# Layer 1's seven-product blocks: readers of another engine's sums issued later, weight sums and splits issued earlier

## The chip, the cores and the metric

One core of a Trainium2 chip. The metric is the device time of one execution in microseconds; the time before is the median of three runs. The profile is of one execution, taken by the hardware profiler.

## The reference

Attention with a hash mask over q, k, v (2 x 8 heads, 768 tokens, 64 wide), then two feed-forward layers in float32. What the change touches is the first of them:

```python
gate = 1.0 / (1.0 + np.exp(-(x @ w_gate)))   # x: 1536 x 512, w_gate: 512 x 1536
val = x @ w_val                               # w_val: 512 x 1536
return (gate * val @ w_out)                   # w_out: 1536 x 512
```

The second layer computes h = x @ w_in, g = h * cos(h), and g @ w_out. All weights arrive as float64.

## The kernel before

**Numbers.** A float32 product is made of three matmuls on rounded parts (high x high, high x low, low x high). So each operand is split: ScalarE casts the high part (L120), and VectorE or GpSimd subtracts it from the operand (L121, the tiles that end in `l`). `convert_parts` turns a weight's float64 words into float32: a ScalarE multiplication (L148, `wp`) and three VectorE instructions (L150, L154, L164).

**Layer 1.** The 1536 hidden columns are 12 blocks f of 128, the tokens three chunks c of 512 (tiles `xy`). g and v are the gate's and the value's weights, o and z the output weights of the two layers. Blocks 0 and 1 are computed plainly (items `in`). The other ten are taken in pairs p = 1 to 5 (f = 2p and 2p+1): for g and then for v, chunks 0 and 1 of both blocks come from seven products M1 to M7 instead of eight, and chunk 2 from two plain ones, P0 and P1. The nine steps follow in the order M1 M5 M2 M6 M3 P0 M7 P1 M4. M1 to M4 read tokens (M4 reads chunk 1's first half, which has been overwritten by a sum), M5, M6, M7 read sums of tokens (tiles T1, T2, T3) and sums of weights (`s12`, `s34`; split tiles `s0..`, `s1..`). Each product is six matmuls of 512 columns, P0 and P1 are twelve. Steps P0 and P1 of g are followed by an `out` item each (twelve matmuls, `a<-gh/gl,o_..`), which multiplies the finished chunk 0 of the pair before with its output weights.

**After a product.** `step` adds a product to running sums: M1 and M5 are copied out of PSUM by ScalarE; c11 = M2 + M1; u = M6 + M1; q = u + M5, then q + M3; u + M7, then M5's tile + u (GpSimd); u + M4. Each finished sum goes to `gate` (ScalarE's sigmoid) for g, or to `value` for v (L836: VectorE multiplies it with the gate). Names in the profile: `M1tg`, `M5tv`, `qg` are these sums; `g<-P1v,g` is `value` reading a product in PSUM.

**Buffers.** The products go round four PSUM banks (`bank`): a step needs the bank of the step four before it, that is its reader. Split weights have four buffers for each role.

**Order.** The program is recorded item by item and keeps that order on every engine; each engine runs its queue in order. `due[n]` lists what is issued ahead of item n: conversions, splits (`wsplit`, `ssplit`), weight sums (`wsum`, GpSimd), loads, spills, and the splits of finished chunks for the output items (`gsplit`, tiles `gh`, `gl`). `before(n, mm)` gives the item that lies mm matmuls ahead of n, `lead` these distances for a weight: first that of its conversion, then that of its split.

**Layer 2** is computed plainly (`PLAIN[2] = 8`). After the items with c = 0 each layer has passes over its output items for c = 1 and 2, with chunks that were spilled to DRAM and are fetched again.

Of the kernel before, what the change touches and what calls it, by code (L numbers as in the profile page):

```python
# [39 lines left out]
def lsh_attention_glu_moe_cos_moe(  # L40
# [663 lines left out]
    def moe():  # L704
        with ExitStack() as st:
# [32 lines left out]
            def wsum(nm, p):  # L738
                w0, w1 = wt.pop((nm, 2 * p, 0)), wt.pop((nm, 2 * p + 1, 0))
# [19 lines left out]
            t4 = {}  # L759
# [7 lines left out]
            def tsplit(h, lw, src, sub):  # L767
                split(h, lw, src, sub)

            def tsum3(l, k, eng, sub):  # L770
                a, b = temp(f"ta{l}{k}"), temp(f"tb{l}{k}")
                eng.tensor_tensor(out=a, in0=x32(1, 0, 2 + k), in1=x32(1, 0, k), op=ALU.subtract)
                eng.tensor_tensor(out=b, in0=x32(1, 1, 2 + k), in1=x32(1, 1, k), op=ALU.subtract)
                eng.tensor_tensor(out=a, in0=a, in1=b, op=ALU.add)
                split(tt[l, 3][:, 0, k, :], tt[l, 3][:, 1, k, :], a, sub)

            def tsum1(l, k, eng, sub):
                a, b = temp(f"tc{l}{k}"), temp(f"td{l}{k}")
                eng.tensor_tensor(out=a, in0=x32(1, 0, k), in1=x32(0, 0, k), op=ALU.subtract)
                eng.tensor_tensor(out=b, in0=x32(1, 1, k), in1=x32(0, 1, k), op=ALU.subtract)  # L780
                eng.tensor_tensor(out=a, in0=a, in1=b, op=ALU.add)
                split(tt[l, 1][:, 0, k, :], tt[l, 1][:, 1, k, :], a, sub)
                eng.tensor_tensor(out=b, in0=x32(1, 0, 2 + k), in1=a, op=ALU.subtract)
                eng.tensor_tensor(out=b, in0=b, in1=x32(1, 1, 2 + k), op=ALU.add)
                split(tt[l, 2][:, 0, k, :], tt[l, 2][:, 1, k, :], b, sub)
                eng.tensor_tensor(out=a, in0=x32(0, 0, 2 + k), in1=b, op=ALU.subtract)
                eng.tensor_tensor(out=a, in0=a, in1=x32(0, 1, 2 + k), op=ALU.add)
                t4[l, k] = a

            def tsum4(l, k, sub):  # L790
                split(xy[1][:, 0, k, :], xy[1][:, 1, k, :], t4.pop((l, k)), sub)
# [76 lines left out]
            st_t = {}  # L868

            def step(n, name, l, nm, p, fill):  # L870
# [37 lines left out]

                if name in ("M1", "M5"):
                    st_t[name] = temp(f"{name}t{nm}{p}")  # L910
                    nc.scalar.copy(st_t[name], ps)
                elif name == "M2":
                    t = temp(f"c11{nm}{p}")
                    plus(nc.vector, t, ps, st_t["M1"])
                    after(t, f0, 0)
                elif name == "M6":
# [3 lines left out]
                    plus(nc.gpsimd, t, u, st_t["M5"])  # L920
                elif name == "M3":
                    t = st_t["q"]
                    plus(nc.vector, t, ps, t)
                    after(t, f0, 1)
                elif name == "M7":
# [3 lines left out]
                    after(t, f1, 1)  # L929
                elif name == "M4":  # L930
                    u = st_t["M1"]
                    plus(nc.vector, u, ps, u)
                    after(u, f1, 0)
# [78 lines left out]
            release = dict(split_at)  # L1012
            for n, (kind, l, f, c) in enumerate(items):
# [10 lines left out]
                elif kind == "M1":  # L1024
                    m = before(n, 36)
                    for f_ in (2 * c, 2 * c + 1):
                        release[f, f_, 0] = m
                    assert all(split_at[f, x, 0] <= m for x in (2 * c, 2 * c + 1))
            for kk in sorted(order, key=lambda kk: begin[use[kk]] - lead(kk)[1]):
                due[split_at[kk]].append(lambda kk=kk: wsplit(kk))  # L1030
            for n, (kind, l, f, c) in enumerate(items):
# [97 lines left out]
```

## Time and profile before

| | |
|---|---|
| median of 3 runs | 889.86 us (885.63 to 890.15) |
| the profiled execution | 892.29 us, its span 890.5 us |
| TensorE busy, in the span | 811.0 us (91%) |
| VectorE | 671.6 us (75%) |
| ScalarE | 489.0 us (55%) |
| GpSimd | 442.5 us (50%) |
| mean granted TensorE clock | 0.966 of full |

The first 270 us are attention; the c = 0 items of the first layer follow to about 538 us, its output passes to about 613, and the second layer to the end. Matmuls are pipelined and their ends are modelled, so a busy TensorE is not one at its peak. An engine's share is a mean over stages that have different limits.

### The profile page before, as it was taken

What the parts mean: (1) busy time and instruction counts of PE and PEld (TensorE: products, weight loads), DVE (VectorE), ACT (ScalarE), POOL (GpSimd) and SP (SyncE); (2) the same over time, 40 slices, a digit from 0 to 9 for tenths busy, and PEclk for the clock granted to TensorE, in tenths of its full rate; (3) what the DMA queues carried; (4) which work ended last, traced back from release to release, by engine and by line L of the source; (5) the groups of instructions that cost most, each with busy time, mean ns of one, the idle gap of its engine ahead of it and who ended that gap; (6) DMA issues with size and microseconds to landing.
All of it is one profiled execution on the core that took longest, in us unless ns stands there. A gap on an engine that the chain in (4) does not pass through costs nothing.

```text
span 890.5 us, 12055 instructions
## 1 busy us (share of the span) xinstructions
PE 811.0 (91%) x3924; PEld 675.5 (76%) x3924; DVE 671.6 (75%) x1060; ACT 489.0 (55%) x944; POOL 442.5 (50%) x409
## 2 busy tenths in 40 slices
PE   6999999999998597787979799999899999989997
PEld 4998889888986485575757577887788888867885
DVE  6999999999965656666666648778777777777774
ACT  5888878888963243242332243445566666654443
POOL 5778877978657576474747452222222222212221
PEclk8999999999998899899989799999999999999999
DMA  6887666676211132313232324553444444447552
GB/s 150 193 222 154 161 163 166 164 168 157 64 27 36 48 107 64 102 48 121 68 119 71 119 71 166 194 177 104 142 145 148 150 147 143 153 168 250 199 177 95
DMA packets 85199, 118.44 MB, mean 133 GB/s; under 512 B 31312, under 2 KB 53840, under 8 KB 85136
## 3 DMA queue, kind: packets, MB, share of 16 engines
q1 hardware_dynamic: 80352, 112.75, 43.5%
q10 hardware_dynamic: 4784, 4.92, 1.8%
q8 instruction: 31, 0.51, 0.2%
q14 instruction: 32, 0.26, 0.1%
HBM read 74.45 MB, written 17.83 MB: 104 GB/s over the span
## 4 chain that ended last, share of the span: by engine, by line
PE 55%; DVE 26%; POOL 7%; issue 5%; ACT 5%; DMA 1%; SPq 0%; DVEq 0%; POOLq 0%; ACTq 0%
PE ph L810 13%; PE a L991 13%; PE a L964 7%; DVE mn L447 4%; PE t L505 4%; DVE pl L515 3%; PE s L436 2%; PE s L439 2%; PE o L526 2%; PE o L525 2%; DVE gl L121 2%; DVE g L836 2%; DVE wl_o L154 1%; DVE w_o L164 1%; DVE w_v L164 1%
## 5 line engine op out<-in xcount | busy, mean ns | idle before, releaser
L489 POOL TENSOR_SCALAR p<-p,r,d 128x768 f32<-128x768 f32 x96 | 97.0, 1015 | 45.8 <-DVE r L480 35.5
L510 ACT CAST ph<-t 128x384 fp32r<-128x384 f32 x192 | 92.4, 485 | 26.2 <-PE t L505 18.0
L515 DVE TENSOR_TENSOR pl<-t,ph 128x384 fp32r<-128x384 f32 x192 | 99.5, 545 | 5.0 <-ACT ph L510 3.4
L447 DVE TENSOR_REDUCE mn<-s 128x1 f32<-128x768 f32 x96 | 90.8, 946 | 10.8 <-PE s L439 10.7
L505 PE MATMUL t<-ident,p 128*128 128x128 f32 x576 | 95.4, 274 | 1.3 <-POOL p L489 1.0
L454 ACT ACTIVATE p<-s,mn 128x768 f32<-128x768 f32 x96 | 87.8, 914 | 6.4 <-DVE mn L447 6.0
L505 PEld LDWEIGHTS t<-ident,p 128*128 128x128 f32 x576 | 74.9, 141 | 10.1 <-DVE bf L400 2.0
L525 PE MATMUL o<-ph,vs 128*128 128x384 f32 x192 | 78.9, 411 | 0.3 <-ACT e L534 0.3
L120 ACT CAST gh<-r 128x512 fp32r<-128x512 f32 x56 | 34.8, 622 | 79.8 <-PE a L991 45.0
L436 PE MATMUL s<-k,q 96*128 96x384 f32 x192 | 71.9, 374 | 2.2 <-ACT p L454 1.6
L526 PE MATMUL o<-pl,vs 128*128 128x384 f32 x192 | 66.3, 345 | 2.5 <-DVE pl L515 2.0
L439 PE MATMUL s<-k,q 128*128 128x384 f32 x192 | 66.6, 347 | 0.0
L843 ACT ACTIVATE n<-ph,quarter 128x512 int32<-128x512 f32 x48 | 33.0, 687 | 59.9 <-PE ph L810 59.7
L121 DVE TENSOR_TENSOR gl<-r,gh 128x512 fp32r<-128x512 f32 x56 | 41.8, 747 | 29.6 <-ACT gh L120 29.5
L845 DVE SCALAR_TENSOR_TENSOR g<-ph,n 128x512 f32<-128x512 f32 x48 | 33.1, 690 | 21.7 <-ACT n L843 21.6
L851 DVE TENSOR_TENSOR g<-ph,g 128x512 f32<-128x512 f32 x48 | 33.0, 688 | 16.9 <-ACT g L850 16.9
L526 PEld LDWEIGHTS o<-pl,vs 128*128 128x128 f32 x192 | 36.8, 191 | 5.9 <-DVE pl L515 5.8
L436 PEld LDWEIGHTS s<-k,q 96*128 96x128 f32 x192 | 37.6, 196 | 3.5 <-ACT p L454 2.7
L850 ACT ACTIVATE g<-g,halfpi 128x512 f32<-128x512 f32 x48 | 34.6, 720 | 7.8 <-DVE g L845 7.8
L525 PEld LDWEIGHTS o<-ph,vs 128*128 128x128 f32 x192 | 36.8, 192 | 1.7 <-ACT e L534 1.7
L439 PEld LDWEIGHTS s<-k,q 128*128 128x128 f32 x192 | 37.7, 196 | 0.0
L154 DVE SCALAR_TENSOR_TENSOR wl_o<-wp_o,wl_o 128x512 int32<-128x512 int32 x24 | 19.6, 819 | 17.8 <-ACT wp_o L148 16.1
(927 smaller groups left out, 2419.2 us busy)
## 6 DMA issues: line engine op xcount, KB each, us to landing
raw_z<-in_moe_w_out SPq DMA_DIRECT2D x32, 512.0 KB, 3.8
d<-g SPq DMA_DIRECT2D x56, 256.0 KB, 3.3
r<-d SPq DMA_DIRECT2D x56, 256.0 KB, 4.0
raw_o<-in_moe_w_out SPq DMA_DIRECT2D x22, 512.0 KB, 3.4
q<-x SPq DMA_DIRECT2D x45, 192.0 KB, 3.1
k<-x SPq DMA_DIRECT2D x45, 192.0 KB, 3.4
raw_i<-in_moe_w_in SPq DMA_DIRECT2D x16, 512.0 KB, 4.3
raw_v<-in_moe_w_val SPq DMA_DIRECT2D x9, 512.0 KB, 3.5
```

Source lines behind the costliest of these rows:

```text
L436: nc.tensor.matmul(o, hh["q2"][0:96, t, :], hh["k2"][0:96, sl, :], start=True, stop=False)
L439: nc.tensor.matmul(o, hh["q1"][:, t, :], hh["k1"][:, sl, :], start=False, stop=True)
L447: nc.vector.tensor_reduce(mn_t[u][:, i : i + 1], s_t[g], axis=AX.XY, op=ALU.min)
L454: nc.scalar.activation(pt, s_t.pop(g), AF.Exp, bias=mn_t[u][:, i : i + 1], scale=-1.0, accum_out=sm_t[u][:, i : i + 1],)
L489: nc.gpsimd.tensor_scalar(out=pt, in0=pt, scalar1=r[:, i : i + 1], scalar2=d[:, i : i + 1], op0=ALU.mult, op1=ALU.add,)
L505: nc.tensor.transpose(pt[:, i, :], pv_[:, j * P : (j + 1) * P], ident)
L510: nc.scalar.copy(ph, pt_t[w])
L515: nc.vector.tensor_tensor(out=pl, in0=pt_t.pop(w), in1=ph_t[w].bitcast(F32), op=ALU.subtract)
L525: nc.tensor.matmul(o_t[u], vs[:, j, :], ph_t.pop(w), start=(j == 0), stop=False)
L526: nc.tensor.matmul(o_t[u], vs[:, j, :], pl_t.pop(w), start=False, stop=(j == T - 1))
L810: nc.tensor.matmul(ps, w[:, kt, :], xy[c][:, hl, kt, :], start=(n == 0), stop=(n == 11))
L991: nc.tensor.matmul(acc[c, t], m[:, ts], w, start=(f == 0 and n == 0), stop=(f == F2 - 1 and n == 2),)
```

## The change

1. **Readers later** (`after` with `wait`, `far`, `post`): the gate of M2, M3, M4 is issued one item later; the gate or value of M7's second sum, which GpSimd adds, three items later.
2. q = u + M5 is added by VectorE instead of GpSimd.
3. **Weights earlier**: conversions of paired weights lead by 150 or 138 matmuls (before 120, 108, 90, 78), splits by 84 or 60 (before 52, 44), weight sums by 100 (36), their splits by 72 and 48 (30, 22). The split of a weight releases its tile now, the sum only reads it.
4. Conversions are put first in each item's list (`early`), in both layers.
5. The sums of tokens (`tsums`) are issued in four stages at items of their own, the splits of a stage after the sums of it, for the two halves k = 0 (GpSimd) and k = 1 (VectorE).

```diff
         if paired(key):
             odd = f % 2
-            return (120 - 12 * odd if nm in "gv" else 90 - 12 * odd), 52 - 8 * odd
+            return 150 - 12 * odd, (60 if odd else 84)
...
-                w0, w1 = wt.pop((nm, 2 * p, 0)), wt.pop((nm, 2 * p + 1, 0))
+                w0, w1 = wt[nm, 2 * p, 0], wt[nm, 2 * p + 1, 0]
...
+                return (
+                    (sum3, sum1),
+                    (lambda: parts(3), sum2),
+                    (lambda: parts(1), lambda: parts(2), sum4),
+                    (lambda: parts(4),),
+                )
...
-                def after(src, f, c):
+                def after(src, f, c, wait=0):
                     if nm == "i":
                         cosine(n, src, f, c, fill)
+                    elif wait:
+                        post.setdefault(n + wait, []).append(lambda: use_it(n + wait, src, f, c))
                     else:
                         use_it(n, src, f, c)
...
+                far = int(nm == "g")
...
-                    after(t, f0, 0)
+                    after(t, f0, 0, far)
...
-                    plus(nc.gpsimd, t, u, st_t["M5"])
+                    plus(nc.vector, t, u, st_t["M5"])
...
                     plus(nc.gpsimd, t, u, t)
-                    after(t, f1, 1)
+                    after(t, f1, 1, 3)
...
+            for n, (kind, l, f, c) in enumerate(items):
+                if kind == "M1":
+                    due[before(n, 100)].append(lambda f=f, c=c: wsum(f, c))
+                    due[before(n, 72)].append(lambda f=f, c=c: ssplit(f, c, 0))
+                    due[before(n, 48)].append(lambda f=f, c=c: ssplit(f, c, 1))
...
-                due[n].append(lambda k=k: convert_to(k + 1))
+                m = before(use[kk], 100) if paired(kk) else split_at[kk]
+                assert n <= m, (kk, n, m, order[k - NEARLY])
+                early[n].append(lambda k=k: convert_to(k + 1))
+            due = [a + b for a, b in zip(early, due)]
...
+                    if l == 1:
+                        slots = (6, 7, 8, 9) if k else (3, 5, 7, 9)
...
+                    for fn in post.pop(n, ()):
+                        fn()
```

**First place: VectorE at the end of the second pair and in g of the third.** Rows are in the order of issue; names as above, the last numbers being the program's. Before, from the sum of M7v to the split of an output item's chunk:

```order
L907 TENSOR_TENSOR M1tv_5003<-M7v_5109,M1tv_5003 128x512
L836 TENSOR_TENSOR g_1_5_4949<-M5tv_5012,g_1_5_4949 128x512
L150 TENSOR_SCALAR wl_v_5124<-raw_v_5071 128x512
L154 SCALAR_TENSOR_TENSOR wl_v_5124<-wp_v_5122,wl_v_5124 128x512
L164 SCALAR_TENSOR_TENSOR w_v_5127<-raw_v_5071,wl_v_5124 128x512
L836 TENSOR_TENSOR g_2_5_4972<-P1v_5130,g_2_5_4972 128x512
L907 TENSOR_TENSOR M1tv_5003<-M4v_5146,M1tv_5003 128x512
L836 TENSOR_TENSOR g_0_5_4994<-M1tv_5003,g_0_5_4994 128x512
L907 TENSOR_TENSOR c11g_5185<-M2g_5178,M1tg_5167 128x512
L907 TENSOR_TENSOR M1tg_5167<-M6g_5189,M1tg_5167 128x512
L121 TENSOR_TENSOR gl_0_4_5200<-g_0_4_4847,gh_0_4_5199 128x512
```

Of the change, from the sum of M4v (ahead of it stand the sum of M7v and the value of P1v, with nothing between them):

```order
L920 TENSOR_TENSOR M1tv_5015<-M4v_5149,M1tv_5015 128x512
L847 TENSOR_TENSOR g_0_5_5017<-M1tv_5015,g_0_5_5017 128x512
L847 TENSOR_TENSOR g_1_5_5006<-M5tv_5039,g_1_5_5006 128x512
L150 TENSOR_SCALAR wl_g_5178<-raw_g_5060 128x512
L154 SCALAR_TENSOR_TENSOR wl_g_5178<-wp_g_5176,wl_g_5178 128x512
L164 SCALAR_TENSOR_TENSOR w_g_5181<-raw_g_5060,wl_g_5178 128x512
L920 TENSOR_TENSOR c11g_5204<-M2g_5197,M1tg_5170 128x512
L150 TENSOR_SCALAR wl_g_5210<-raw_g_5108 128x512
L154 SCALAR_TENSOR_TENSOR wl_g_5210<-wp_g_5208,wl_g_5210 128x512
L164 SCALAR_TENSOR_TENSOR w_g_5213<-raw_g_5108,wl_g_5210 128x512
L920 TENSOR_TENSOR M1tg_5170<-M6g_5219,M1tg_5170 128x512
L920 TENSOR_TENSOR qg_5227<-M1tg_5170,M5tg_5194 128x512
```

The next row is `gl_0_4`. The product with M5tv has moved behind M4v's, the v conversion away, and two g conversions and the q add stand ahead of `gl`.

**Second place: VectorE ahead of the first pair**, from the token sums of T3 on. Before:

```order
L774 TENSOR_TENSOR ta_4371<-ta_4371,tb_4372 128x512
L121 TENSOR_TENSOR T_1_4259<-ta_4371,T_1_4259 128x512
L779 TENSOR_TENSOR tc_4378<-xy_69,xy_68 128x512
L780 TENSOR_TENSOR td_4379<-xy_69,xy_68 128x512
L781 TENSOR_TENSOR tc_4378<-tc_4378,td_4379 128x512
L121 TENSOR_TENSOR T_1_4257<-tc_4378,T_1_4257 128x512
```

Of the change, from the value of item (1, 1):

```order
L847 TENSOR_TENSOR g_1_1_4465<-pv_1_4440,g_1_1_4465 128x512
L150 TENSOR_SCALAR wl_g_4473<-raw_g_4342 128x512
L154 SCALAR_TENSOR_TENSOR wl_g_4473<-wp_g_4471,wl_g_4473 128x512
L164 SCALAR_TENSOR_TENSOR w_g_4476<-raw_g_4342,wl_g_4473 128x512
L150 TENSOR_SCALAR wl_g_4482<-raw_g_4367 128x512
L154 SCALAR_TENSOR_TENSOR wl_g_4482<-wp_g_4480,wl_g_4482 128x512
L164 SCALAR_TENSOR_TENSOR w_g_4485<-raw_g_4367,wl_g_4482 128x512
L121 TENSOR_TENSOR T_1_4275<-ta_4429,T_1_4275 128x512
L785 TENSOR_TENSOR td_4435<-xy_69,tc_4434 128x512
L786 TENSOR_TENSOR td_4435<-td_4435,xy_69 128x512
L847 TENSOR_TENSOR g_2_1_4532<-pv_1_4507,g_2_1_4532 128x512
L121 TENSOR_TENSOR T_1_4273<-tc_4434,T_1_4273 128x512
```

The last row of both pieces is T1's low part, which M5 reads. Values and two g conversions have moved between the sums and it.

**Third place: VectorE in the output pass of layer 1**, at blocks f = 5 and 6 (gl_c_f). Before:

```order
L121 TENSOR_TENSOR gl_1_5_6411<-r_1_5_6347,gh_1_5_6410 128x512
L150 TENSOR_SCALAR wl_o_6424<-raw_o_6322 128x512
L154 SCALAR_TENSOR_TENSOR wl_o_6424<-wp_o_6422,wl_o_6424 128x512
L164 SCALAR_TENSOR_TENSOR w_o_6427<-raw_o_6322,wl_o_6424 128x512
L121 TENSOR_TENSOR gl_2_5_6442<-r_2_5_6365,gh_2_5_6441 128x512
```

Of the change:

```order
L150 TENSOR_SCALAR wl_o_6414<-raw_o_6312 128x512
L154 SCALAR_TENSOR_TENSOR wl_o_6414<-wp_o_6412,wl_o_6414 128x512
L164 SCALAR_TENSOR_TENSOR w_o_6417<-raw_o_6312,wl_o_6414 128x512
L121 TENSOR_TENSOR gl_1_5_6420<-r_1_5_6347,gh_1_5_6419 128x512
L121 TENSOR_TENSOR gl_2_5_6442<-r_2_5_6374,gh_2_5_6441 128x512
```

The conversion has moved from between the two splits to ahead of the first.

## Rows read from the trace of the kernel before

**Rows 1.** Stretches: busy time by engine, instructions, granted clock, DMA share, GB/s.

```profile
316.64:351.93 35.29, 30.38 (x134) 24.55 (x132) 21.71 (x26) 13.97 (x25) 24.27 (x21) 1.00 0.23 75
351.93:400.20 48.27, 40.29 (x157) 31.65 (x157) 30.93 (x37) 15.53 (x28) 28.07 (x23) 0.90 0.28 87
400.20:447.67 47.47, 38.10 (x157) 30.11 (x157) 30.98 (x37) 15.53 (x28) 28.08 (x23) 0.96 0.28 89
447.67:494.88 47.21, 39.49 (x156) 30.94 (x157) 30.96 (x37) 15.54 (x28) 28.07 (x23) 0.93 0.28 90
```

**Rows 2.** Waits of TensorE, 316.6 to 538.6: total us, times, longest.

```profile
PE M2g L891 <- DVE g L836: 15.0, 4, 3.9
PE M1g L891 <- DVE g L836: 10.2, 4, 2.9
PE a L964 <- DVE gl L121: 4.9, 3, 1.8
...
PE M6v L891 <- DVE M1tg L907: 1.1, 1, 1.1
```

**Rows 3.** TensorE in order of time: start, us, instruction, [idle before <-releaser].

```profile
308.30 1.22 PE L810 MATMUL pg<-xy,g_1h 128*128 128x512 f32 x2 [8.92 <-ACT g L831]
...
331.60 0.62 PE L891 MATMUL M1v<-xy,v_2h 128*128 128x512 f32 x2
...
360.38 1.22 PE L891 MATMUL M2g<-xy,g_4h 128*128 128x512 f32 x2 [3.75 <-DVE g L836]
...
523.66 0.61 PE L891 MATMUL M1v<-xy,v_10h 128*128 128x512 f32 x2
...
525.02 0.61 PE L891 MATMUL M5v<-T,s0v5h 128*128 128x512 f32 x2
```

**Rows 4.** VectorE in order of time, end of the first pair.

```profile
354.03 0.68 DVE L907 TENSOR_TENSOR M1tv<-M7v,M1tv 128x512 f32<-128x512 f32 x1
356.11 1.75 DVE L836 TENSOR_TENSOR g<-M5tv,g 128x512 f32<-128x512 f32 x1 [1.40 <-POOL M5tv L907]
357.79 0.41 DVE L150 TENSOR_SCALAR wl_v<-raw_v 128x512 int32<-128x512 int32 x1
358.30 0.69 DVE L154 SCALAR_TENSOR_TENSOR wl_v<-wp_v,wl_v 128x512 int32<-128x512 int32 x1
359.03 0.69 DVE L164 SCALAR_TENSOR_TENSOR w_v<-raw_v,wl_v 128x512 int32<-128x512 int32 x1
359.64 0.68 DVE L836 TENSOR_TENSOR g<-P1v,g 128x512 f32<-128x512 f32 x1
```

**Rows 5.** VectorE's groups, 351.9 to 494.9: busy, mean ns, idle before.

```profile
L164 DVE SCALAR_TENSOR_TENSOR w_g<-raw_g,wl_g 128x512 int32<-128x512 int32 x6 | 8.4, 1394 | 0.2
...
L150 DVE TENSOR_SCALAR wl_g<-raw_g 128x512 int32<-128x512 int32 x6 | 5.8, 964 | 0.0
...
L154 DVE SCALAR_TENSOR_TENSOR wl_g<-wp_g,wl_g 128x512 int32<-128x512 int32 x6 | 5.5, 919 | 6.2 <-ACT wp_g L148 5.9
```

**Rows 6.** GpSimd's groups, 351.9 to 494.9: busy, mean ns, idle before.

```profile
L907 POOL TENSOR_TENSOR qg<-M1tg,M5tg 128x512 f32<-128x512 f32 x3 | 4.8, 1601 | 26.0 <-DVE M1tg L907 26.0
L907 POOL TENSOR_TENSOR M5tv<-M1tv,M5tv 128x512 f32<-128x512 f32 x3 | 3.9, 1291 | 7.5 <-DVE M1tv L907 7.5
...
L121 POOL TENSOR_TENSOR v_4l<-w_v,v_4h 128x512 fp32r<-128x512 f32 x1 | 1.7, 1743 | 0.0
```

**Rows 7.** VectorE in order of time, after M4g of the second pair.

```profile
382.92 0.69 DVE L907 TENSOR_TENSOR M1tg<-M4g,M1tg 128x512 f32<-128x512 f32 x1 [3.75 <-PE M4g L891]
...
387.27 1.33 DVE L154 SCALAR_TENSOR_TENSOR wl_o<-wp_o,wl_o 128x512 int32<-128x512 int32 x1 [2.64 <-ACT wp_o L148]
```

**Rows 8.** VectorE in order of time, at layer 1's start.

```profile
274.62 0.69 DVE L121 TENSOR_TENSOR gl<-g,gh 128x512 fp32r<-128x512 f32 x1 [0.68 <-ACT gh L120]
```

**Rows 9.** VectorE in order of time, in the output pass.

```profile
560.82 0.68 DVE L121 TENSOR_TENSOR gl<-r,gh 128x512 fp32r<-128x512 f32 x1
562.68 0.69 DVE L121 TENSOR_TENSOR gl<-r,gh 128x512 fp32r<-128x512 f32 x1 [1.18 <-ACT gh L120]
```

More of the change, by code (lines that the diff above doesn't have):

```diff
@@ L758, in moe @@
             tt = {}
-            t4 = {}
             def temp(name):
@@ L765, in x32 @@
                 return xy[c][:, hl, k, :].bitcast(F32)
[L767 to L788, printed above, removed]
@@ L790, in tsum4, with tsums, sum3, sum1 @@
-            def tsum4(l, k, sub):
-                split(xy[1][:, 0, k, :], xy[1][:, 1, k, :], t4.pop((l, k)), sub)
+            def tsums(l, k, eng, sub):
+                tw = {}
+                def sum3():
+                    a, b = temp(f"ta{l}{k}"), temp(f"tb{l}{k}")
+                    eng.tensor_tensor(out=a, in0=x32(1, 0, 2 + k), in1=x32(1, 0, k), op=ALU.subtract)
+                    eng.tensor_tensor(out=b, in0=x32(1, 1, 2 + k), in1=x32(1, 1, k), op=ALU.subtract)
+                    eng.tensor_tensor(out=a, in0=a, in1=b, op=ALU.add)
+                    tw[3] = a
+                def sum1():
+                    a, b = temp(f"tc{l}{k}"), temp(f"td{l}{k}")
+                    eng.tensor_tensor(out=a, in0=x32(1, 0, k), in1=x32(0, 0, k), op=ALU.subtract)
+                    eng.tensor_tensor(out=b, in0=x32(1, 1, k), in1=x32(0, 1, k), op=ALU.subtract)
+                    eng.tensor_tensor(out=a, in0=a, in1=b, op=ALU.add)
+                    tw[1], tw[2] = a, b
+                def sum2():
+                    a, b = tw[1], tw[2]
+                    eng.tensor_tensor(out=b, in0=x32(1, 0, 2 + k), in1=a, op=ALU.subtract)
+                    eng.tensor_tensor(out=b, in0=b, in1=x32(1, 1, 2 + k), op=ALU.add)
+                def sum4():
+                    a, b = tw[1], tw[2]
+                    eng.tensor_tensor(out=a, in0=x32(0, 0, 2 + k), in1=b, op=ALU.subtract)
+                    eng.tensor_tensor(out=a, in0=a, in1=x32(0, 1, 2 + k), op=ALU.add)
+                def parts(i):
+                    t = xy[1] if i == 4 else tt[l, i]
+                    split(t[:, 0, k, :], t[:, 1, k, :], tw[1 if i == 4 else i], sub)
+                return (
[4 more added lines that the diff above has]
+                )
@@ L923, in step @@
                     plus(nc.vector, t, ps, t)
-                    after(t, f0, 1)
+                    after(t, f0, 1, far)
                 elif name == "M7":
@@ L932, in step @@
                     plus(nc.vector, u, ps, u)
-                    after(u, f1, 0)
+                    after(u, f1, 0, far)
                 else:
@@ L1012, in moe @@
             release = dict(split_at)
+            early = [[] for _ in due]
             for n, (kind, l, f, c) in enumerate(items):
@@ L1024, in moe @@
                 elif kind == "M1":
-                    m = before(n, 36)
+                    m = before(n, 100)
                     for f_ in (2 * c, 2 * c + 1):
-                        release[f, f_, 0] = m
-                    assert all(split_at[f, x, 0] <= m for x in (2 * c, 2 * c + 1))
+                        release[f, f_, 0] = max(m, split_at[f, f_, 0])
+            for n, (kind, l, f, c) in enumerate(items):
[3 more added lines that the diff above has]
+                    due[before(n, 48)].append(lambda f=f, c=c: ssplit(f, c, 1))
             for kk in sorted(order, key=lambda kk: begin[use[kk]] - lead(kk)[1]):
                 due[split_at[kk]].append(lambda kk=kk: wsplit(kk))
-            for n, (kind, l, f, c) in enumerate(items):
-                if kind == "M1":
-                    due[before(n, 36)].append(lambda f=f, c=c: wsum(f, c))
-                    due[before(n, 30)].append(lambda f=f, c=c: ssplit(f, c, 0))
-                    due[before(n, 22)].append(lambda f=f, c=c: ssplit(f, c, 1))
             for k, kk in enumerate(order[NEARLY:], NEARLY):
                 n = max(before(use[kk], lead(kk)[0]), release[order[k - NEARLY]])
-                assert n <= split_at[kk], (kk, n, split_at[kk], order[k - NEARLY])
-                due[n].append(lambda k=k: convert_to(k + 1))
+                m = before(use[kk], 100) if paired(kk) else split_at[kk]
+                assert n <= m, (kk, n, m, order[k - NEARLY])
+                early[n].append(lambda k=k: convert_to(k + 1))
+            due = [a + b for a, b in zip(early, due)]
             V, G = nc.vector, nc.gpsimd
```

18 lines of the change are left out of this document (7 added, 11 removed).

## The prediction

> **What bounds the kernel now.** I read the stretches first. Behind 316.64 us lies the part of the first layer that is made of seven-product blocks, cut at each pair's first matmul (M1g), the last pair beginning at 494.88 [rows 1]. Matmuls of 512 columns follow each other at 0.227 us at full clock: six take 1.36 us, from 523.66 to 525.02 [rows 3]. A pair with its two output items is 156 matmuls, 35.4 us; the three middle pairs take 48.27, 47.47 and 47.21 us [rows 1], so 12 us of each is lost. TensorE's busy time there is 40.29 us in the first of them: 8.0 us is idle and about 4.9 us goes to the lower clock level (the granted clock is 0.90 of full). The list of waits says where the idle time is: M2g and M1g wait for VectorE's L836 (`value`), 15.0 and 10.2 us in four goes each, and output items wait for `gl` [rows 2]. These are waits for PSUM banks. Four banks go round, so M1g needs the bank of P0v, M5g that of M7v, M2g that of P1v.
>
> VectorE's order shows why they come free late. After M7v's sum it stands 1.40 us until GpSimd has added M5tv, then runs that product in 1.75 us, then a weight conversion (three instructions, L150, L154, L164), and only at 359.64 reads P1v [rows 4]; M2g starts at 360.38, and at half speed, 1.22 us for two matmuls against 0.61 [rows 3, 4]. GpSimd itself comes late to M5tv since weight sums and splits stand ahead of it. Outside these blocks the bound is TensorE at full clock, but for a wait of 8.92 us at 308.30, where the gate of an earlier product stood on ScalarE behind the token sums [rows 3].
>
> **The change at the end of a pair.** I walk VectorE's new order (the first place in the section on the change). Let S be the end of M1tv<-M7v. GpSimd now comes to M5tv at once (1.29 us [rows 6]), since its weight sums are issued 100 matmuls ahead instead of 36; VectorE reads P1v meanwhile, then M4v's sum, which waits for GpSimd: S+2.1. So M1g, M5g and M2g of the next pair find their banks free, and the 25.2 us of [rows 2]'s first two rows, with the clock behind them, go. But what stood in front of the banks now stands in front of `gl`. Behind M4v's sum come two products with both inputs in SBUF (1.1 us each, between 0.69 alone and 1.75 as g<-M5tv measured [rows 4]), one g conversion, c11, a second g conversion, M6's sum, the new q add and then gl of the output item. A g conversion is 0.96+0.92+1.39 = 3.28 us by its three rows [rows 5], 3.5 with gaps; the same three alone take about 1.85 (0.41, 0.69, 0.69 and gaps [rows 4]). I take 3.5, since GpSimd works through s_v's sums and v's splits all that while. The sum: 2.1+2.2+3.5+0.6+3.6+0.6+1.3+1.2 = S+15.1. TensorE starts M1g at S-1.0 and wants that gl 43 matmuls later, at S+8.75. **A new wait of about 6.3 us, once in a pair, in the output item.** Behind a wait of that length I expect some 5 us at the lower clock, 2.4 us lost, half of the 4.9 that the first middle pair loses with two or three waits; bounds 0 and 4.9.
>
> From gl to the end of M4g lie 47 matmuls: 10.65+2.4 = 13.05 us. From M4g's end to the next S VectorE has its sum (0.7), a v conversion whose second instruction waits for ScalarE's `wp` (now behind a sigmoid and the copy of M1v, 3.2 us after M4g's end; before, 387.27-382.92 = 4.35 [rows 7]), an o conversion, and then, with GpSimd mostly idle, conversions of 1.85 and eight instructions at 0.6 to 0.7: 5.0, 7.8, 9.1, 11.0, 14.3, 16.2, and S' at 16.8. P1v loses 0.75 us to M6's late sum. **A middle pair: 15.1+13.05+16.8 = 45.0 us, against 47.65 in the mean: three pairs give 7.9 us.** The q add moved from GpSimd (1.6 us and a round trip) to VectorE is in this sum with 1.3 us in g and 0.7 in v; ScalarE's gates that come an item later (`far`) cost nothing, the work behind them being ready.
>
> **The last pair** (p = 5) has no g conversion ahead of its gl: 2.1+2.2+0.6+0.6+1.3+1.2 = S+8.0, in time for S+8.75. From M1g to M1v 90 matmuls, 20.4 us, against 523.66-494.88 = 28.8 [rows 1, 3]: 8.4 us. The wait of M6v, 1.1 us [rows 2], goes as well.
>
> **The first pair.** M1v ran at 331.60 and the next M1g at 351.93 [rows 1, 3], 20.3 us; by the walk above 15.8: 4.5 us.
>
> **The start costs time.** (1) A conversion now stands between the first value and its gl (274.62 [rows 8]): +1.5 us, bounds 0.4 and 3.3. (2) The second place: the gate of item (1,1) stands on ScalarE behind s1g1's cast, which takes g_1's buffer and so waits for the last product with g_1. That frees the banks in time for M1g, so the 8.92 us wait goes. But M5g needs the token sums T1, and on VectorE these now stand behind two g conversions (7.1 us), a split, two adds of 1.7 each, a value and T1's own split: 13.3 us behind that value. The value: the product ahead of the old wait ended at 308.30-8.92 = 299.4; with 1.5 us of (1), 2.7 for the last product with g_1, and cast, gate and value at 0.6 to 0.7, 305.7. M5g starts near 319, eleven us after M1g ended, and at the lower clock; M4g ends near 335.0, where before M1v began at 331.60. Together **+3.4 us**, bounds 0 and +8. (3) One g conversion moves into attention, whose VectorE is nearly full: its L150 and L154, 1.9 us at most, +1 taken, bounds 0 and 1.9.
>
> **The output passes of c = 1, 2.** Conversions now come first in each item's list: the place of the conversion moves from between gl_1 and gl_2 to ahead of gl_1 (third place). VectorE idles 1.18 us before one gl of every two [rows 9], and the other was made behind a conversion already; 0 taken. The same holds for the second layer. DMA: each weight load is issued two conversions ahead and the late spill stands ahead of loads that are wanted 20 us later; 0.
>
> **Sum.** +1+3.4-4.5-7.9-8.4-1.1 = -17.5 us. The profiled execution took 892.29 us (span 890.5 and 1.8 around it), 0.3% above the median of 889.86; against the median 872.4. I predict **872 us**.
>
> **A rule weighed.** g<-M5tv took 1.75 us where GpSimd ran, a VectorE instruction of its size 0.69 alone; GpSimd's split took 1743 ns, its sum of M5tv 1291 [rows 4, 6]. So both are slowed, VectorE by about a microsecond. The Trainium skill (SBUF — State Buffer, SBUF: two separate sides) says that a VectorE instruction with two SBUF inputs and one of GpSimd take the shared port pair as an exclusive lock, and that the loser is blocked for the whole instruction. By that rule each of the instructions ahead of gl would wait out a whole GpSimd instruction, and the change would lose: the second rival prices this. The trace agrees on the blocking, and not on its full length.
>
> **Rivals.** The forecast, a gain of 12 to 24 us: 0.5.
> - *The walk is too dark*: little contention (a conversion 2 us, adds 0.7), so gl comes at S+10.5, the wait is under 2 us, the clock stays up, and a middle pair takes 38 us. 21 us more, 851. For it: v's L154 and L164 took 0.69 us each in the same trace [rows 4]. Against it: the g conversions fall just where GpSimd has no pause. 0.2.
> - *The port takes it back*: each of the eight contended instructions ahead of gl (g0, g1, L154 and L164 twice, q, gl) costs 1.65 to 1.75 us, as the slowest rows do; gl at S+18.5, a pair takes 48.4, and the start loses 3 us more. Gain 17.5-10.2-3 = 4 us, 886; with half of it 11 us, 879. For it: M5tv's row. Against it: the L154 rows mean 0.9, the L164 rows 1.4 [rows 5]. 0.15. Were each to wait out a whole GpSimd instruction, 1.29+0.69 = 1.98 us, and the two L150 too, gl would come at S+22.5, a pair would take 52.4, and the time would be 898: 0.03, since no row of VectorE is that long.
> - *The output passes turn over* (slower): gl_1 behind a conversion comes late in each pair of items. There are some 27 of these pairs in the two layers; from 0.8 us in each the gain of 17.5 is gone and 4.4 more, the measure's grain. For it: gl ends at 561.50, within a microsecond of its use. Against it: that gl stood behind a conversion too, and 1.18 us were left. 0.04, 894 and above.
> - *It doesn't do what it says*: GpSimd still comes late to M5tv, M4v's sum waits for it and M6g takes M2g's place; two or three us in each of four pairs and the start's cost: gain about 4, 886. Against it: its queue is empty for some 10 us before. 0.08.
>
> Half a per cent, 4.4 us, is what a measurement of this kernel can tell from no change: 885.4 and 894.3 are the borders. Slower are the output passes and the full port, 0.07; the same is half of the port's 0.15 and a little of the last rival, 0.10; faster is the rest, 0.83. The range, 854 to 885, runs from the bright walk's 851 nearly to where the port takes it back; a little under 0.1 is left out below and about the same above.
>
> **What would show it.** M1g and M2g wait for nothing in pairs 2 to 5; in their place `a<-gl` waits 5 to 7 us in pairs 2, 3 and 4 and not in 5; periods near 45, the last from M1g to M1v near 20.5. M5g of the first pair waits about 11 us. VectorE's g conversions mean 3.3 us or more. The output passes keep 5.44 us for two items. It is wrong if the period is below 41 or above 47, if the first pair's M5g comes before 314 or after 324, or if gl waits appear behind 540 us.

## The result, and the profile after

The changed kernel takes 876.62 us (median of four runs, 874.7 to 878.45), the kernel before 890.0 (four runs, 885.63 to 890.24): ratio 0.9861, interval 0.9823 to 0.9898, some 12 us faster by that ratio (9 to 16), 13.4 by the medians. 872 was forecast, in a range of 854 to 885. Its profiled execution took 874.70 us, span 872.9.

The stretches between the first matmuls (M1g) of the pairs, and at the end from the last M1g to M1v, answer to [rows 1] (busy time of TensorE, its weight loads, VectorE, ScalarE, GpSimd, granted clock, DMA):

```profile
304.90:348.88 43.98, 33.76 (x134) 25.78 (x132) 35.14 (x39) 16.96 (x31) 27.56 (x22) 0.88 0.28 85
348.88:393.69 44.81, 37.81 (x157) 30.29 (x156) 31.01 (x39) 15.31 (x28) 24.43 (x20) 0.92 0.29 97
393.69:438.28 44.59, 37.57 (x158) 30.14 (x156) 31.00 (x39) 15.30 (x28) 24.39 (x20) 0.92 0.29 95
438.28:484.40 46.12, 39.10 (x158) 31.19 (x156) 31.00 (x39) 15.31 (x28) 24.40 (x20) 0.93 0.27 92
484.40:505.04 20.64, 20.64 (x92) 16.81 (x90) 15.51 (x19) 9.03 (x16) 15.46 (x12) 1.00 0.23 80
```

The middle pairs take 44.8, 44.6 and 46.1 us instead of 47 to 48, the last 20.64 without a gap. TensorE's waits in this part answer to [rows 2]:

```profile
PE a L978 <- DVE gl L121: 14.4, 3, 4.8
PE P1v L821 <- DVE M1tv L920: 5.6, 4, 1.5
PE M5g L902 <- POOL T L121: 4.8, 1, 4.8
PE a L978 <- ACT gh L120: 2.6, 3, 0.9
PE M5g L902 <- DVE T L121: 2.3, 1, 2.3
PE M5g L902 <- ACT T L120: 1.5, 1, 1.5
```

M1g and M2g no longer stand in the list. In their place the first output item of pairs 2, 3 and 4 waits for `gl`, and P1v waits 1.4 us in each of four pairs for M6v's sum. VectorE between M7v's sum and that `gl`, in the second pair (answers to [rows 4]):

```profile
349.22 0.68 DVE L920 TENSOR_TENSOR M1tv<-M7v,M1tv 128x512 f32<-128x512 f32 x1
349.82 0.68 DVE L847 TENSOR_TENSOR g<-P1v,g 128x512 f32<-128x512 f32 x1
351.31 0.69 DVE L920 TENSOR_TENSOR M1tv<-M4v,M1tv 128x512 f32<-128x512 f32 x1 [0.81 <-POOL M5tv L920]
...
353.80 0.96 DVE L150 TENSOR_SCALAR wl_g<-raw_g 128x512 int32<-128x512 int32 x1
354.87 1.04 DVE L154 SCALAR_TENSOR_TENSOR wl_g<-wp_g,wl_g 128x512 int32<-128x512 int32 x1
355.94 1.66 DVE L164 SCALAR_TENSOR_TENSOR w_g<-raw_g,wl_g 128x512 int32<-128x512 int32 x1
357.53 0.68 DVE L920 TENSOR_TENSOR c11g<-M2g,M1tg 128x512 f32<-128x512 f32 x1
...
360.75 1.64 DVE L164 SCALAR_TENSOR_TENSOR w_g<-raw_g,wl_g 128x512 int32<-128x512 int32 x1
362.31 0.68 DVE L920 TENSOR_TENSOR M1tg<-M6g,M1tg 128x512 f32<-128x512 f32 x1
363.02 1.03 DVE L920 TENSOR_TENSOR qg<-M1tg,M5tg 128x512 f32<-128x512 f32 x1
363.98 0.68 DVE L121 TENSOR_TENSOR gl<-g,gh 128x512 fp32r<-128x512 f32 x1
```

P1v is read right behind M7v's sum, as intended. From the end of that sum, 349.90, to the end of `gl`, 364.66, it is 14.8 us, of which the two g conversions are about 8. The other gaps of TensorE are in the first pair, where M5g waits three times, and in attention, where TensorE waits 4.2 us for the split tile `pl` behind a VectorE instruction that waits for its output buffer and has no counterpart before. M5g's first and last wait, then TensorE's wait in attention and the row of VectorE:

```profile
307.92 0.51 PE L902 MATMUL M5g<-T,s0g1h 128*128 128x512 f32 x1 [1.50 <-ACT T L120]
317.16 0.79 PE L902 MATMUL M5g<-T,s0g1h 128*128 128x512 f32 x1 [2.26 <-DVE T L121]
...
PE o L526 <- DVE pl L515: 4.2, 1, 4.2
...
252.67 1.73 DVE L164 SCALAR_TENSOR_TENSOR w_g<-raw_g,wl_g 128x512 int32<-128x512 int32 x1 [3.56 <-POOL v_0l L121]
```

### The profile page after: what moved, and what is told of

Same layout as the page of the kernel before. It is cut to its first block, busy times and chain, and to the rows that moved or that the text cites. A ratio compares the mean times of both kernels' runs of the same rounds, so it can differ in the third digit from the quotient of the medians.

```text
span 872.9 us, 12027 instructions
## 1 busy us (share of the span) xinstructions
PE 804.0 (92%) x3924; PEld 670.9 (77%) x3924; DVE 653.1 (75%) x1070; ACT 488.9 (56%) x944; POOL 429.2 (49%) x399
## 4 chain that ended last, share of the span: by engine, by line
PE 62%; DVE 26%; issue 4%; ACT 3%; DMA 2%; POOL 1%; SPq 0%; DVEq 0%; ACTq 0%; POOLq 0%
PE ph L821 14%; PE a L1005 14%; PE a L978 10%; DVE mn L447 4%; PE t L505 4%; DVE pl L515 4%; PE s L436 2%; PE s L439 2%; PE o L526 2%; PE o L525 2%; PE P1g L821 2%; DVE w_g L164 2%; DVE gl L121 2%; DVE g L847 1%; DVE wl_g L154 1%
## 5 line engine op out<-in xcount | busy, mean ns | idle before, releaser
L342 POOL TENSOR_TENSOR x<-xf,x 128x384 fp32r<-128x384 f32 x28 | 30.0, 1070 | 2.3
```

## The experiments

The theory was that VectorE's order sets everything: what stands ahead of a bank's reader makes M1g and M2g wait, what stands ahead of `gl` makes the output item wait. The rivals: GpSimd's late sums, contention wherever a conversion stands, and a VectorE that is simply full. Each kernel was timed in three rounds beside the kernel before (medians 888.5 to 890.2).

### Which part freed the banks

**1. The kernel before with the later reads alone** (part 1 of the change).

```diff
-                    after(t, f1, 1)
+                    after(t, f1, 1, 3)
```

and `far` for the gates, with `post`, as in the change. 

> The kernel before, with the later reads alone. The theory, that VectorE's order is what held the banks: 1.4 us of standing for GpSimd and the product of 1.75 us no longer lie ahead of the read of P1v, M2g's wait falls from 3.7 us to about 1 in each of four pairs, M1g's wait of 2.5 us stays; a pair takes 44 to 45 us instead of 47.6, and the time falls by 8 to 14 us, to 876 to 882. The rival, that GpSimd comes late because its weight sums are issued late, and that the later reads only move the wait: within 4 us of the kernel before, 886 to 894.

Measured: 872.84 us, ratio 0.9807 (0.9779 to 0.9835); pairs of 44.4 us. Faster than the theory and the rival said, and at least as fast as the whole change. TensorE's waits in the pairs:

```profile
PE M1g L891 <- DVE g L836: 10.8, 4, 3.5
PE M2g L891 <- DVE g L836: 9.8, 4, 2.5
PE a L967 <- DVE gl L121: 0.7, 3, 0.2
```

M2g's 15.0 us [rows 2] fell by a third only, since a v conversion still stands ahead of P1v's read; but M4v's sum, c11g and `gl` behind it come sooner too, and the wait for `gl` (4.9 before) is nearly gone. The rival on GpSimd's late sums falls. The trace of before speaks against it too: GpSimd stood idle and began M5tv 0.08 us after M7v's sum had ended (354.71 [rows 4]).

```profile
354.79 1.28 POOL L907 TENSOR_TENSOR M5tv<-M1tv,M5tv 128x512 f32<-128x512 f32 x1 [2.49 <-DVE M1tv L907]
```

**2. The same, with q on VectorE** (parts 1 and 2).

```diff
-                    plus(nc.gpsimd, t, u, st_t["M5"])
+                    plus(nc.vector, t, u, st_t["M5"])
```

> The kernel before, with the later reads and the sum q on VectorE, leads and order as before. In the run with the later reads alone (872.8 us) M1g still waits 2.4 to 3.5 us for the read of P0v and M2g 2.4. The theory, that 0.7 us of this is GpSimd's round trip for q in v: M1g waits some 0.7 us less, a pair takes 43.5 to 44 us instead of 44.4, gl 1 us more; 868 to 872. The rival: the add costs VectorE in g what it saves in v, and the time stays within 1 us, 872 to 874. If the leads and not these two parts carried the gain, it would be above 880; the run with the later reads alone speaks against that already.

Measured: 865.43 us, ratio 0.9735 (0.9708 to 0.9762). M1g's waits went from 10.8 to 7.8 us, by 0.75 in each of four pairs (the theory had 0.7), and M2g's from 9.8 to 8.7:

```profile
PE M2g L891 <- DVE g L836: 8.7, 4, 2.6
PE M1g L891 <- DVE g L836: 7.8, 4, 2.4
```

The three middle periods sum to 128.8 us (42.9 each), a larger gain than the theory's. So **two of the five parts give 24 us, and the other three together take 11 of them back.**

**3. The change without part 1.**

```diff
-                far = int(nm == "g")
+                far = 0
...
-                    after(t, f1, 1, 3)
+                    after(t, f1, 1)
```

> The changed kernel with the later reads undone: gates and values of GpSimd's and VectorE's sums are issued with their product again, all else as changed. The theory, that the order on VectorE frees the banks: it stands 1.4 us for GpSimd's sum of M5tv, runs that product, and reads P1v at 3.3 us behind the sum of M7v, so M2g waits 1.5 to 2 us in each of four pairs; in pairs 2 to 4 this lies mostly under the wait for gl, which comes about 0.6 us later. 2 to 5 us slower than the changed kernel, 879 to 882. The rival, that the later reads carry the gain: M1g and M2g wait 2 us and more each again, and 10 us or more are lost, 887 or above.

Measured: 878.32 us, ratio 0.9871 (0.9849 to 0.9894). M2g waits 1.4 us in each of four pairs, and the waits for `gl` and `gh` shrink from 17.0 to 12.9 us. TensorE's waits:

```profile
PE a L978 <- DVE gl L121: 8.4, 3, 2.8
PE M2g L902 <- DVE g L847: 5.7, 4, 1.4
PE a L978 <- ACT gh L120: 4.5, 3, 1.5
```

The part that is worth 17 us alone is worth 1.7 here, inside the spread of the runs: the wait for `gl` stands in the same half of the pair and covers it.

**4. The change without part 2** (q back on GpSimd).

```diff
-                    plus(nc.vector, t, u, st_t["M5"])
+                    plus(nc.gpsimd, t, u, st_t["M5"])
```

> The changed kernel with the sum q = u + M5 given back to GpSimd. The theory: in v the round trip of 1.4 us stands in VectorE's order again in place of an add of 0.7, so the sum of M7v and with it the next pair come 0.7 to 1.4 us later; in g an add of 1.0 us ahead of gl goes. Together 0 to 5 us slower, 877 to 882. The rival: the order ahead of gl alone counts, and the kernel gets 2 to 3 us faster, 873 to 875.

Measured: 874.82 us (873.2 to 879.0), ratio 0.9839 (0.9805 to 0.9874): not told apart from the changed kernel. The longest wait for `gl` is 2.8 us instead of 4.8, as the rival said, and the v half of a pair keeps its length (16.61 us from M1v at 378.34 to M1g at 394.95, with q on VectorE 16.63). Part 2 gave 7 us in experiment 2, with the conversions where they stood before; here it gives nothing that can be told from the spread.

### What the new wait is

**5. The g conversions behind `gl`.**

```diff
-            return 150 - 12 * odd, (60 if odd else 84)
+            return (120 if nm == "g" else 150) - 12 * odd, (60 if odd else 84)
```

> The changed kernel, with one number altered: the conversions of the paired g weights lead by 120 and 108 matmuls instead of 150 and 138, so that VectorE runs them behind the split gl of the pair's first output item instead of ahead of it. The theory, that what stands ahead of gl on VectorE sets the wait: gl ends about 7 us behind the sum of M7v instead of 14.8, in time for its use, the waits of 4.8 us in pairs 2, 3 and 4 go and the clock stays up; a pair takes 37 to 39 us instead of 44.8; the two conversions ahead of T1 go too, so the first product M5 comes 2 to 4 us sooner. 851 to 858 us against 876.6. The rival, contention with GpSimd wherever the conversions stand: they hold up the second gl and the sum of M7g instead, a pair takes 42 us or more, and the time is above 866.

Measured: 853.7 us, ratio 0.9592 (0.9568 to 0.9615). The lead of 120 (108 for the odd block) is the kernel before's own. The wait for that `gl` is gone, 1.3 us are left at the second output item's, a pair takes 38.9 us, at full clock (the third pair's stretch, columns as above):

```profile
385.26:424.16 38.90, 36.26 (x157) 29.04 (x156) 31.46 (x39) 15.76 (x28) 24.32 (x20) 1.00 0.32 109
```

The sum of M7v ends at 386.30 there and `gl` at 395.08, 8.8 us behind it and just in time. One number, and 23 us. Of the 21.3 us between the two profiled spans 18.9 lie in the three middle pairs: there the order ahead of `gl` was the bound. 3.3 us lie ahead of the first M1v, where the first pair's two g conversions moved too.

**6. The change without the sums of the v weights on GpSimd** (for v, `wsum` and `ssplit` return at once, and `step` takes the plain split weights in their place, so the products M5, M6 and M7 of v are others).

```diff
+                if nm == "v":
+                    return
...
-                    s12, s34 = (nm, p, "s", 0), (nm, p, "s", 1)
+                    s12, s34 = (a0, a1) if nm == "v" else ((nm, p, "s", 0), (nm, p, "s", 1))
```

> The changed kernel without the sums of the v weights: the four sums, their two splits and casts of each pair are left out, and v's products that use them take the plain split weights, so the output is another. VectorE's instructions and their order stay. In pairs 2 to 4 GpSimd then is free for some 8 us of the stretch in which the two g conversions ahead of gl run. The theory, that these conversions take 3.7 and 4.1 us instead of 1.9 because GpSimd works beside them: one of them or both fall to about 2 us, gl comes 12 us behind the sum of M7v instead of 14.8, a pair takes 41 to 43 us instead of 44.8, and the time is 865 to 870. The rival, that they are slow for another reason: the pairs keep 44.5 to 45 us, and the time is within 2 us of 876.6.

Measured: 865.18 us, ratio 0.9734 (0.972 to 0.9749); pairs of 42.5 to 42.8 us. VectorE's groups over the three middle pairs (busy, mean ns of one), of the changed kernel:

```profile
L164 DVE SCALAR_TENSOR_TENSOR w_g<-raw_g,wl_g 128x512 int32<-128x512 int32 x6 | 9.9, 1650 | 0.2
L154 DVE SCALAR_TENSOR_TENSOR wl_g<-wp_g,wl_g 128x512 int32<-128x512 int32 x6 | 7.8, 1308 | 0.6
...
L150 DVE TENSOR_SCALAR wl_g<-raw_g 128x512 int32<-128x512 int32 x6 | 5.6, 935 | 0.0
...
L920 DVE TENSOR_TENSOR c11g<-M2g,M1tg 128x512 f32<-128x512 f32 x3 | 2.0, 676 | 0.0
```

and of this run:

```profile
L154 DVE SCALAR_TENSOR_TENSOR wl_g<-wp_g,wl_g 128x512 int32<-128x512 int32 x6 | 4.2, 693 | 0.6
L164 DVE SCALAR_TENSOR_TENSOR w_g<-raw_g,wl_g 128x512 int32<-128x512 int32 x6 | 4.2, 692 | 0.2
...
L150 DVE TENSOR_SCALAR wl_g<-raw_g 128x512 int32<-128x512 int32 x6 | 2.5, 414 | 0.0
```

A conversion falls from 3.9 to 1.8 us (the sum of the three means) with nothing changed in VectorE's instructions and their order: its length is GpSimd's doing. `gl` comes 12.6 us behind M7v's sum instead of 14.8; part of the gift is lost, since `gl` itself and the product with M5tv now meet GpSimd's splits (1289 and 1774 ns).

### The start

**7. Only the first pair's g conversions later.**

```diff
+            return (120 if nm == "g" and f < 4 else 150) - 12 * odd, (60 if odd else 84)
```

> The changed kernel, but the two g weights of the first pair alone are converted 120 and 108 matmuls ahead instead of 150 and 138; the other pairs as changed. In the changed kernel's trace VectorE stands 3.56 us at L164 of the first of these conversions at 252.67 us, in attention, since its buffer comes free with GpSimd's split v_0l, and TensorE stands 4.2 us for pl behind it; the prediction had put 1 us on this term. The theory, that this conversion holds attention up: that wait goes, the first output item comes at about 271 us instead of 274, the first M5 another 1 to 3 us sooner, since a conversion less stands ahead of T1, and the pairs keep their 44.8 us. 868 to 873 us against 876.6. The rival, that the term was rightly sized and attention varies by that much in any case: 874 or above.

Measured: 874.39 us, ratio 0.9828 (0.9809 to 0.9847): a miss for the theory's number (868 to 873), just inside the rival's (874 or above), though not for the theory's first step. VectorE's 3.56 us in attention are gone, the first output item starts at 271.07 instead of 273.60, M1g at 300.50 instead of 304.90. But the three waits of M5g grow from 8.6 to 11.5 us. TensorE in order of time:

```profile
304.75 0.51 PE L902 MATMUL M5g<-T,s0g1h 128*128 128x512 f32 x1 [2.72 <-ACT T L120]
310.07 0.80 PE L902 MATMUL M5g<-T,s0g1h 128*128 128x512 f32 x1 [4.82 <-POOL T L121]
315.65 0.79 PE L902 MATMUL M5g<-T,s0g1h 128*128 128x512 f32 x1 [3.93 <-DVE T L121]
```

and the first M1v comes 0.9 us sooner, while M1g comes 4.4 sooner. What comes early in attention waits at the sums of tokens.

**8. The order of the tokens' sums** (on top of experiment 9): T1 ahead of T3.

```diff
-                    (sum3, sum1),
-                    (lambda: parts(3), sum2),
-                    (lambda: parts(1), lambda: parts(2), sum4),
+                    (sum1, sum3),
+                    (lambda: parts(1), sum2),
+                    (lambda: parts(2), lambda: parts(3), sum4),
...
-                        due[base + m].extend(fns)
+                        due[base + m][0:0] = fns
```

> As the run before, and the sums of tokens in the order of their use: T1 is summed and split ahead of T2 and T3, and each stage is put first in its item's list instead of last. The theory, that the first M5 waits for T1 only because T3's sums, the v weights' sums and splits stand ahead of it on VectorE, GpSimd and ScalarE: of its 7.6 us of waits 5 or more go, some of it comes back at M6, which needs T2; 4 to 7 us off, 840 to 846. The rival, that the sums take as long in any order, so that M6 or M7 waits instead: within 2 us of the run before.

Measured: 854.03 us, ratio 0.9603 (0.9583 to 0.9623), no better than experiment 9. M5g has one wait instead of three (8.0 us together in experiment 9), and that is for a bank. TensorE in order of time:

```profile
309.16 1.22 PE L902 MATMUL M5g<-T,s0g1h 128*128 128x512 f32 x2 [7.21 <-DVE g L847]
```

VectorE's read of that bank (`g`) stands behind T3's sum, which waits for a buffer. VectorE in order of time:

```profile
305.10 1.74 DVE L772 TENSOR_TENSOR tb<-xy 128x512 f32<-128x512 f32 x1 [8.87 <-POOL T L121]
```

The sums take eight temporary tiles of a pool of six (`temp`, `bufs=6`); the new order keeps them longer. A larger pool was not tried. The time is 2.6 us above experiment 9's, near the rival's 2, by another wait than the rival's.

### A version that beats both

**9. Leads set by VectorE's order.**

```diff
-            return 150 - 12 * odd, (60 if odd else 84)
+            return ((96 if odd else 120) if nm == "g" else (138 if odd else 156)), (60 if odd else 84)
```

with 96 instead of 100 for the weight sums. 

> The changed kernel with the leads set by the order on VectorE: g conversions 120 and 96 matmuls ahead (behind the first and behind the second gl of the pair), the first v conversion 156 instead of 150 (an item earlier, so that ScalarE's wp_v is not behind the copy of M1v), sums of weights 96 instead of 100. The theory: the wait for gl goes as in the run with later g conversions (853.7 us), and what was left there goes too: the second gl's 1.3 us, and P1v's 1.35 us, which comes from VectorE standing 1.7 us for wp_v. A pair takes 36 to 37.5 us against 38.9, and the time is 845 to 850. The rival, that VectorE, busy 31 us of a pair, has no room left and the waits only move: 38.5 us and more, 852 or above.

Measured: 851.46 us, ratio 0.9576 (0.9561 to 0.959): nearer the rival. The third pair's g and v half (columns as above):

```profile
384.44:405.08 20.64, 20.64 (x92) 16.82 (x90) 18.34 (x19) 8.99 (x16) 16.74 (x14) 1.00 0.23 81
405.08:422.82 17.74, 15.56 (x67) 12.23 (x66) 16.03 (x20) 6.53 (x12) 8.42 (x7) 1.00 0.43 143
```

The g half now takes 20.64 us, its 90 matmuls and nothing else. The v half keeps 17.7: VectorE is busy 34.4 us of the pair's 38.4, its v and o conversions meet GpSimd's splits, and M7v and P1v wait.

**10. The same with the later reads undone.**

```diff
-                far = int(nm == "g")
+                far = 0
...
-                    after(t, f1, 1, 3)
+                    after(t, f1, 1)
```

> The run with the leads set by VectorE's order (851.5 us), with the later reads undone. The theory, that in the changed kernel the later reads were worth only 1.7 us because the wait for gl covered the bank waits: without that cover M2g waits 1.4 us in each of four pairs and VectorE stands 1.4 us for GpSimd's sum, so it gets 3 to 7 us slower, 854 to 859. The rivals: the later reads are worth nothing wherever conversions are out of the way, 853 or less; or the bank waits return in full, 3 us and more each, 862 or above.

Measured: 860.64 us, ratio 0.9686 (0.9654 to 0.9718), 9.2 us slower, above the theory's 3 to 7. TensorE's waits in the pairs:

```profile
PE P1v L821 <- DVE M1tv L920: 5.7, 4, 1.5
PE M2g L902 <- DVE g L847: 5.7, 4, 1.4
PE M7v L902 <- DVE c11v L920: 4.8, 3, 1.6
PE M2v L902 <- ACT g L842: 2.4, 1, 2.4
```

M2g's 1.4 us is as forecast; the rest is in v, where VectorE stands 2.37 us for `wp_v`, in experiment 9 0.79. In this run ScalarE's gate of M4g's sum stands ahead of `wp_v`, so the later gates on ScalarE count here as well. The same part is worth 17, 1.7 or 9 us, by what else stands in VectorE's order.

**11. On top of experiment 9: o conversions out of v, the first `gl` earlier, the old order in the output passes.**

```diff
+        if nm == "o" and f >= 2 * PLAIN[1] and f < F1 - 2:
+            return (72 if f % 2 else 66), 40
...
-                    m = max(m, n - 2)
+                    m = max(m, n - (6 if l == 1 and c == 0 and f % 2 == 0 and 2 <= f < F1 - 2 else 2))
...
-            due = [a + b for a, b in zip(early, due)]
+            late = at["out", 1, 0, 1] - 4
+            due = [a + b if n < late else b + a for n, (a, b) in enumerate(zip(early, due))]
```

> The run with the leads set by VectorE's order, with three more moves: the two o conversions of a pair go out of the way of c11 and the sums of M6v and M7v (leads 66 and 72 instead of 96: behind the product with P0v, and behind M4v's), the first gl of a pair is issued before the product with M5tv, and in the output passes conversions stand behind the splits again, as before the change. The theory: in the v half VectorE's order alone sets the pace (M7v waits 0.7 us for c11v, P1v 1.5 us for M6v's sum); with the o conversions away v takes 15 to 16.3 us instead of 17.75 and a pair 36 to 37 us instead of 38.4; the waits for gl at the start of the output pass, 2.7 us, go. 839 to 845 us against 851.5. The rival, that VectorE with 34 us of work in a pair has no room left: what v gains, g loses to gl or to the banks, and the time is 848 or above.

Measured: 846.13 us, ratio 0.9514 (0.949 to 0.9539), a little outside the theory. v falls to 15.6 us, as it said, but g rises to 22.45, with a wait of 1.75 us for the second `gl`: a pair takes 38.1 us against 38.4: what v gains g loses, as the rival said of the pairs. The rest came from the output passes (from the last M1v to the end 365.6 us against 367.8) and the first pair.

**12. On top of experiment 11: the second `gl` earlier too.**

```diff
-                    m = max(m, n - (6 if l == 1 and c == 0 and f % 2 == 0 and 2 <= f < F1 - 2 else 2))
+                    m = max(m, n - ((5 if f % 2 else 6) if l == 1 and c == 0 and 2 <= f < F1 - 2 else 2))
```

> The run of 846.1 us with one more move: the split gl of a pair's second output item is issued three items earlier, ahead of the sum of M3g and of the first g conversion, so that ScalarE's cast gh and VectorE's split of it no longer stand behind them. The theory: its wait of 1.75 us in each of four pairs goes and nothing takes its place, since the bank of M3g is wanted two items later; a pair takes 36.2 to 36.8 us instead of 38.1, and the time is 839 to 843 us. The rival, that VectorE is full by now: the sums of M7g and M4g come later by as much and v loses what g gains, a pair takes 37.5 us or more, and the time is above 844.5.

Measured: 845.04 us, ratio 0.9501 (0.9469 to 0.9532): the rival's time (above 844.5), and not told apart from experiment 11. No wait for `gl` is left in the pairs and g takes 20.40 us; one pair takes 36.5, but the ones beside it 39.5, where VectorE stands 2.36 us for `wp_v` (1.49 in the short one) and P1v waits 2.07 (0.77). Why they alternate stays open. These two are the fastest kernels of the study, this one 5% ahead of the kernel before and 3.6% ahead of the changed one.

## Why the prediction held

**The sum, stretch by stretch** (us, one profiled execution each; M1v and M1g are TensorE's first matmuls of these steps):

| stretch | before | after | measured | forecast |
|---|---|---|---|---|
| start to the first M1v | 331.60 | 331.67 | +0.1 | +4.4 |
| to the second M1g | 20.33 | 17.21 | -3.1 | -4.5 |
| three middle pairs | 142.95 | 135.52 | -7.4 | -7.9 |
| last M1g to last M1v | 28.78 | 20.64 | -8.1 | -8.4 |
| from there to the end | 366.84 | 367.86 | +1.0 | -1.1 |
| span | 890.5 | 872.9 | -17.6 | -17.5 |

**The end of a pair was right, in its steps as well.** M4v's sum ends at S+2.1, as forecast; `gl` at S+14.8 (15.1); the wait is 4.8 us and 0.87 for `gh` (6.3 together); from `gl` to the end of M4g 12.6 us (13.05), from there to the next S 17.5 (16.8, with P1v's wait at 0.75 instead of 1.4); a pair 44.8 us (45.0), the last half 20.64 (20.4). In the last pair `gl` ended at S+8.8, not S+8.0, which is just when it was wanted (S+8.75): that it left no gap had no margin. Experiment 5 shows that the conversions ahead of `gl` cause this wait, experiment 6 that GpSimd sets their length: 3.9 us each where 3.5 was taken.

**A cause in the text was wrong, with no term in the sum.** "GpSimd now comes to M5tv at once ... since its weight sums are issued 100 matmuls ahead": it came at once before too, 0.08 us behind M7v's sum (row in experiment 1), so GpSimd was not late in the kernel before, as the text has it. VectorE's 1.40 us in [rows 4] is the add itself, 1.29 us [rows 6], and in the changed kernel VectorE reads P1v in that time. Experiment 1 gives 17 us with the weight sums where they were.

**The start's terms were mis-sized, and one execution hid it.** The conversion moved into attention was put at +1 (0 to 1.9) as its own instructions; not asked was what its buffer waits for: it waits for GpSimd's v_0l, 3.56 us, and TensorE 4.2 behind it. In the four kernels that have it ahead (the change, experiments 3, 4 and 6) the first output item starts at 273.60 to 274.43, in the nine others at 270.72 to 272.43: 2 to 3 us. That the profile of before has 274.69 is that execution's own: experiments 1 and 2, whose VectorE, ScalarE and GpSimd run the same instructions in the same order up to there, have 271.05 and 272.43. With these in its place the table's +0.1 is +2.3 to +3.7, and the forecast +4.4 was near by luck, with the wrong shares: the rest of the start cost 1.1 us (58.07 us from the first output item to M1v, 56.91 before), not 3.4.

M5g did not wait as a whole, as the walk had it, but in three pieces. The first matmul came at 307.92, and by that the prediction's own sign of being wrong, M5g before 314, was met. The last, which needs T1's low part from VectorE, came at 317.16, 10.7 us behind the end of M1g, where eleven were forecast; the walk had only that one.

**The output passes were taken as 0.** From the last M1v to the end it is 367.1 to 369.5 us in the nine kernels whose conversions stand first there, 363.7 to 366.8 in the five with the old order: 3.0 us in the mean. The rival had the place, and expected it in each pair of items. In the middle of the pass two items keep their 5.44 us; the loss shows where the pass begins, in two waits for `gl` that experiments 1, 2, 11 and 12, with the old order, don't have:

```profile
524.20 0.50 PE L978 MATMUL a<-gl,o_11h 128*128 128x512 f32 x1 [1.09 <-DVE gl L121]
534.25 0.50 PE L978 MATMUL a<-gl,o_1h 128*128 128x512 f32 x1 [1.59 <-DVE gl L121]
```

The prediction's sign of being wrong, `gl` waits behind 540 us, could not tell the two kernels apart: the kernel before has such waits there itself, 2.9 us in six goes in the first layer.

**Why 13 and not 17.5.** The sum was made against the profiled 892.29 us, which lies above every timed run of before (891.48 at most, with the rounds beside the experiments), while the profiled 874.70 is the lowest of the changed kernel's four. Of the difference of 4 us between the two comparisons, 2.3 to 3.6 are that attention of the one execution. That the profiled spans differ by 17.6, as forecast to 0.1, is luck.

**What the prediction did not ask** is what each part is worth alone. Later reads and q give 24 us. Against that kernel (span 863.9) the change has lost 2.3 us up to the first M1v, 6.8 in the middle pairs and 4.1 behind the last, and gained 0.3 and 3.8 in the halves between: 9.0 us of span. In the pairs the loss is the earlier g conversions (experiment 5), behind the last pair the conversions put first. Part 5, the order of the token sums, was not tried by itself.

## What to carry to other kernels

When a wait on the bottleneck engine goes, walk the in-order queue of the engine that had caused it on to the next thing that is wanted from it, and price what was put ahead of that; here two moves made the gain and the earlier conversions lost half of it. Work that is "early" is only free where its engine stands idle: here the same g conversions, issued 30 matmuls later and so behind `gl`, made the kernel 23 us faster. Of a moved instruction ask what frees its output buffer, before its own time is counted.

## What the runs showed of the hardware

That GpSimd slows VectorE was expected, the regularity was not. On 128x512, a g conversion's L154 and L164 take 0.69 us each where GpSimd stands idle beside them (experiment 6) and 1.0 to 1.7 us where it works (the changed kernel); L150, with one input, 414 ns and 935 in the mean; c11g, which reads one of its inputs from a PSUM bank, 676 ns in the same stretch. GpSimd's splits take up to 1.74 us beside them, where its sum of M5tv takes 1.29 [rows 6]. Where both queues are full the two take turns: in about 1.7 us each finishes one instruction, where the two alone would take 0.69 + 1.29 = 1.98 one after the other. That is close to the exclusive lock of the Trainium skill (SBUF — State Buffer, SBUF: two separate sides), which names VectorE instructions that have two SBUF inputs, against a GpSimd instruction that reads SBUF, or run in a two-port mode. These runs agree for L154, L164 and c11g, with 0.3 us of each turn overlapped; whether L150 runs in such a mode no run here shows. The prediction's full lock, 1.98 us for each of the instructions ahead of `gl` and `gl` at S+22.5, did not come: the longest of them took 1.67 us, and only some of the eight meet GpSimd.
